# First mixture: three nested further tiles of an expert instead of six, and the branch hints given to all five engines

## The chip, the cores and the metric

One core of one Trainium2 chip. The metric is the device time of one execution in microseconds (us). Three runs of the kernel before took 1198.63, 1197.80 and 1197.21 us; their median is 1197.8 us. One more execution was taken with the hardware profiler; it is the one whose rows are shown.

## The reference, cut to what matters

```
x   = attention(q, k, v)                 # 4 batches x 576 rows = 2304 tokens of 512 numbers
# first mixture: 8 experts, F = 1024, not every token takes part
on  = x @ w_skip > 0
e   = argmax(x[on] @ w_gate)             # one expert a token
x[on] += gate * relu(x[on] @ w1[e]) @ w2[e]
# second mixture: 4 experts, F = 1024, every token through every expert
p   = domain_probs / sum(domain_probs)
out = sum over e of p[e] * (relu(x @ v1[e]) @ v2[e])
```

With these inputs 807 tokens take part in the first mixture; the eight experts get 7, 9, 127, 179, 459, 16, 2 and 8 of them. In tiles of 128 rows that is one tile for each expert, one further tile for expert 3 and three further tiles for expert 4: twelve tiles in all. The kernel can't know these counts ahead.

## The kernel before, in words

The kernel has three stages: attention and routing, to about 230 us of the profiled execution; the first mixture (`m1`), to about 410 us; and the second mixture, to the end. Every product in fp32 is made of three matmuls of a high and a low part, so ScalarE and VectorE split each operand (`parts`, `w_split`) before TensorE can use it.

**Routing.** Each token that takes part is written to a place in a region `XS` in DRAM, which holds the rows of each expert one behind the other. `counts` (line 489) counts the tokens of each expert on TensorE and works out on VectorE, in `row` (line 154, `[128, CM, 8]` int32), the first row of each further tile c, for c from 1 to CM - 1.

**A tile of the first mixture** (`m1_tile`): the rows of a tile are loaded, turned by four transposes on TensorE (`turned`, line 692), split, multiplied by w1 (line 710) and w2 (line 729), and the result is added to the row by VectorE into `ys` (line 737). GpSimd then writes `ys` to the tokens' places in `XN` by an indirect DMA, the put (line 738). There are two `ys` buffers (`YB = 2`). While a tile runs, `mid` turns and splits the rows of the tile that comes after it.

**The loop over experts** is unrolled. For each expert the first tile always runs. Then `more(1, x1)` opens a nested `tc.If` (line 803): the further tile c runs where the count is above 128 * c, and inside it stands the If of tile c + 1. For c below CM = 6 the further tile first loads the rows of tile c + 1, gives a hint on the next branch and turns those rows in `mid`, whether or not tile c + 1 will run. The tile at c = CM has none of that. Behind it stands a loop, without a hint, for the tiles that are left; with 459 rows it never runs. An expert's way out is thus a taken branch past the code of all further tiles that it doesn't need. Only behind the If comes `out()`, which adds and puts the expert's first tile. So the engines go past each branch in their own time, and meet again where data, or a buffer, is needed.

They tell the engine's sequencer early which way a branch with that label will go. There is one ahead of each first tile and one in each further tile with c below CM.

**Weights.** Weights come by SP's queue through a ring of raw tiles; as soon as a split frees one, the next load starts (`fetch`, `sp`). ScalarE and VectorE split them between the tiles' own work (lines 661 and 662).

## Time and profile before

| | us |
|---|---|
| median of three runs | 1197.8 |
| profiled execution, its own time | 1193.83 |
| its span (first to last instruction) | 1192.2 |
| VectorE's addition into `ys`, first and last start | 254.0 and 409.7 |
| TensorE busy from 443 to 1192 us | 743.43 of 749 |
| TensorE busy over the span | 1108.0 |

The span is from the first to the last instruction of the profiled execution; 1.6 us lie around it. Times in rows are in us from the span's start. PE is TensorE (PEld its weight loads, PEq or PEldq its sequencer, which runs branches and waits), DVE is VectorE, ACT ScalarE, POOL GpSimd, SP SyncE. In a row in order of time the bracket tells how long the engine had been idle and what ended the wait.

### The profile page before, as it was taken

The numbers are of one execution on the slowest core, as the hardware profiler recorded it, in microseconds if no ns is written. First come the engines' busy times: TensorE is split into PE (matmuls) and PEld (weight loads), VectorE is DVE, ScalarE is ACT, GpSimd is POOL, SyncE is SP. The second block draws the span as 40 slices with busy tenths as digits, with TensorE's granted clock in tenths as the row PEclk, the third lists the DMA queues.
The fourth block names the chain that finished last, engine by engine and source line by source line (L and its number), as shares of the span: only waits on it lengthen the run. The fifth ranks groups of instructions, "written<-read, shape, count | busy, mean of one in ns | idle before, by whom it ended". The sixth has DMA issues, their size and how long they took to land.

```text
span 1192.2 us, 19617 instructions
## 1 busy us (share of the span) xinstructions
PE 1108.0 (93%) x7485; PEld 973.3 (82%) x7485; DVE 767.6 (64%) x1227; ACT 505.9 (42%) x827; POOL 577.6 (48%) x579
## 2 busy tenths in 40 slices
PE   5889888699898779999999999999999999999998
PEld 4778887588797668988898998889888888888887
DVE  6767676578525676666666666666866667666665
ACT  5887785376425553332323233322533333333331
POOL 5968775101111065445454444545666555555551
PEclk8998899599999989999999999999999999999999
DMA  5998849499824331111111111111322111111101
GB/s 188 206 204 194 184 111 227 152 316 368 266 91 155 102 133 54 36 36 36 54 36 44 45 37 36 36 54 36 124 72 70 53 54 48 59 36 57 50 1 70
DMA packets 127248, 123.07 MB, mean 103 GB/s; under 512 B 63341, under 2 KB 96109, under 8 KB 127120
## 3 DMA queue, kind: packets, MB, share of 16 engines
q1 hardware_dynamic: 124400, 116.82, 33.8%
q0 software_dynamic: 2720, 4.64, 1.1%
q8 instruction: 69, 1.13, 0.4%
q14 instruction: 59, 0.48, 0.1%
HBM read 91.83 MB, written 19.43 MB: 93 GB/s over the span
## 4 chain that ended last, share of the span: by engine, by line
PE 62%; DVE 3%; POOL 1%; ACT 1%; DMA 0%; issue 0%; SPq 0%; POOLq 0%; ACTq 0%
PE yp L669 11%; PE yp L670 11%; PE yp L668 11%; PE hp L669 9%; PE hp L670 9%; PE hp L668 9%; DVE xsl L872 1%; PE hp L710 1%; PE yp L729 0%; DVE acc L1002 0%; DMA x<-XN 0%; PE tp L854 0%; DVE C L940 0%; POOL C L940 0%; POOL p L940 0%
## 5 line engine op out<-in xcount | busy, mean ns | idle before, releaser
L1002 DVE SCALAR_TENSOR_TENSOR acc<-yp,p,acc 128x512 f32<-128x512 f32 x270 | 199.1, 746 | 108.7 <-PE yp L670 108.6
L947 ACT ACTIVATE hh<-C 128x512 fp32r<-128x512 f32 (+2 forms) x98 | 81.7, 834 | 369.3 <-DVE C L940 328.8
L668 PE MATMUL yp<-vh,hh 128*128 128x512 f32 x576 | 226.6, 393 | 5.1 <-ACT hh L947 4.8
L669 PE MATMUL yp<-vl,hh 128*128 128x512 f32 x576 | 227.2, 394 | 1.0 <-POOL vl L917 1.0
L670 PE MATMUL yp<-vh,hl 128*128 128x512 f32 x576 | 226.4, 393 | 0.3 <-DVE hl L948 0.3
L948 DVE SCALAR_TENSOR_TENSOR hl<-C,hh 128x512 fp32r<-128x512 f32 (+2 forms) x98 | 93.2, 951 | 98.6 <-ACT hh L947 98.6
L940 POOL TENSOR_TENSOR p<-C,p 128x256 f32<-128x256 f32 (+2 forms) x49 | 50.4, 1029 | 199.4 <-ACT p L937 199.4
L670 PEld LDWEIGHTS yp<-vh,hl 128*128 128x128 f32 x576 | 108.7, 189 | 24.9 <-DVE hl L948 1.6
L668 PEld LDWEIGHTS yp<-vh,hh 128*128 128x128 f32 x576 | 109.0, 189 | 23.6 <-ACT hh L947 5.7
L669 PEld LDWEIGHTS yp<-vl,hh 128*128 128x128 f32 x576 | 109.0, 189 | 18.8 <-POOL vl L917 1.8
L917 POOL TENSOR_TENSOR vl<-r,vh 128x512 fp32r<-128x512 f32 x64 | 83.1, 1310 | 79.3 <-ACT vh L914 79.3
L940 DVE TENSOR_TENSOR C<-hp,p 128x256 f32<-128x256 f32 (+2 forms) x147 | 80.0, 544 | 35.6 <-PE hp L670 13.9
L669 PE MATMUL hp<-xsl,th 128*128 128x256 f32 (+2 forms) x294 | 97.9, 333 | 1.5 <-DVE xsl L872 1.5
L668 PE MATMUL hp<-xsh,th 128*128 128x256 f32 (+2 forms) x294 | 97.8, 333 | 0.0
L670 PE MATMUL hp<-xsh,tl 128*128 128x256 f32 (+2 forms) x294 | 97.8, 332 | 0.0
L738 POOL DMA_INDIRECT XN<-ys,xg x10 | 14.7, 1469 | 139.5 <-DVE ys L737 91.2
L302 ACT ACTIVATE E<-s,m 128x320 f32<-128x320 f32 (+4 forms) x160 | 75.9, 532 | 10.6 <-DVE m L295 9.2
L335 POOL TENSOR_TENSOR HL<-E,HL 128x1152 bf16<-128x1152 f32 (+2 forms) x37 | 63.7, 1737 | 21.9 <-ACT HL L334 14.6
L295 DVE TENSOR_REDUCE m<-s 128x1 f32<-128x576 f32 (+3 forms) x80 | 64.9, 819 | 14.1 <-PE s L286 12.6
L940 POOL TENSOR_TENSOR C<-C 128x256 f32<-128x256 f32 (+2 forms) x49 | 52.5, 1070 | 36.1 <-ACT C L937 34.8
L668 PE MATMUL hp<-xdh,dh 128*128 128x256 f32 (+2 forms) x196 | 65.1, 332 | 1.2 <-ACT xdh L861 1.2
L669 PE MATMUL hp<-xdl,dh 128*128 128x256 f32 (+2 forms) x196 | 65.2, 333 | 0.3 <-DVE xdl L862 0.3
(215 smaller groups left out, 2866.6 us busy)
## 6 DMA issues: line engine op xcount, KB each, us to landing
r<-in_w_dram SPq DMA_DIRECT2D x128, 512.0 KB, 5.8
XN<-x SPq DMA_DIRECT2D x18, 256.0 KB, 3.8
vr<-in_v_dram SPq DMA_DIRECT2D x7, 640.0 KB
xg<-XS SPq DMA_DIRECT2D x16, 257.0 KB, 5.7
out_dram<-acc SPq DMA_DIRECT2D x16, 256.0 KB, 2.0
qr<-in_q_dram SPq DMA_DIRECT2D x7, 576.0 KB, 7.4
kr<-in_k_dram SPq DMA_DIRECT2D x7, 576.0 KB, 6.4
x<-XN SPq DMA_DIRECT2D x12, 256.0 KB, 4.0
```

What stands on the lines that cost most here:

```text
L295: nc.vector.tensor_reduce(mo, mi, axis=ax, op=ALU.max, negate=True)
L302: nc.scalar.activation(e, views[j], AF.Exp, bias=m[:R, c:c + 1])
L335: (nc.vector if item[:2] in self.HV else nc.gpsimd).tensor_tensor(HL[:R, w:2 * w].bitcast(BF16), Et[:R, 0:w], HL[:R, 0:w], ALU.subtract)
L668: nc.tensor.matmul(out, lhsT=ah, rhs=bh, start=start, stop=False)
L669: nc.tensor.matmul(out, lhsT=ah, rhs=bl, start=False, stop=False)
L670: nc.tensor.matmul(out, lhsT=al, rhs=bh, start=False, stop=stop)
L738: nc.gpsimd.indirect_dma_start(out=self.XN, out_offset=bass.IndirectOffsetOnAxis(ap=xg[:, DM:DM + 1].bitcast(I32), axis=0), in_=ys, in_off ...
L917: nc.gpsimd.tensor_tensor(vl[:, f], r2[:, f], vh[:, f].bitcast(F32), ALU.subtract)
L940: add = lambda e, o, x, y: e.tensor_tensor(o, x, y, ALU.add)
L947: nc.scalar.activation(hh, C[:, i:i + 2], AF.Relu)
L948: V.scalar_tensor_tensor(hl, C[:, i:i + 2], 0.0, hh.bitcast(F32), ALU.max, ALU.subtract)
L1002: nc.vector.scalar_tensor_tensor(a, yp, self.p[:, n, e:e + 1], a, ALU.mult, ALU.add)
```

## The change

`CM` goes from 6 to 3, and the list of engines that get the hints goes to `None`, which stands for all five engines.

```
-    CM = 6
+    CM = 3
...
-        en = [mybir.EngineType.PE, mybir.EngineType.Activation, mybir.EngineType.DVE]
+        en = None
```

So the program holds, for each expert, the code of a first tile, three nested further tiles and the loop, instead of a first tile, six and the loop. The row tile is `[128, 3, 8]` instead of `[128, 6, 8]`, and `counts` fills two row numbers instead of five. The third further tile is now the one at c = CM: it loads and turns no rows of a fourth, and gives no hint; the test for a fourth tile is now that of the loop, without a hint. GpSimd and SyncE get the instructions of the hints too.

## Rows read from the trace of the kernel before

**Rows 1.** The page, part 1: busy time, share of the span, instructions.

```profile
PE 1108.0 (93%) x7485; PEld 973.3 (82%) x7485; DVE 767.6 (64%) x1227; ACT 505.9 (42%) x827; POOL 577.6 (48%) x579
```

**Rows 2.** Busy time by stretch: PE, PEld, DVE, ACT, POOL; clock, DMA share, GB/s.

```profile
365.10:383.30 18.20, 14.57 (x84) 12.55 (x85) 11.81 (x12) 10.17 (x14) 2.72 (x2) 0.91 0.56 184
443.00:1192.00 749.00, 743.43 (x3764) 645.01 (x3763) 487.25 (x691) 237.41 (x381) 382.12 (x374) 1.00 0.15 49
```

**Rows 3.** Instructions of line 737: count, ns min/median/max, first and last start.

```profile
L737 DVE SCALAR_TENSOR_TENSOR ys<-yp,xg x10: 750/751/752, 254.0 to 409.7; 128x512 f32<-128x512 f32 x10
L737 DVE SCALAR_TENSOR_TENSOR ys<-yp,xi x2: 751/752/752, 351.6 to 364.3; 128x512 f32<-128x512 f32 x2
```

**Rows 4.** TensorE and ScalarE in order: start, us busy, engine, work [idle us before <-releaser].

```profile
252.50 0.35 PE L710 MATMUL hp<-w1h,hi 128*128 128x256 f32 x1 [0.64 <-PEq L803]
280.51 0.38 PE L710 MATMUL hp<-w1h,hi 128*128 128x256 f32 x1 [1.10 <-ACTq L803]
280.80 2.00 ACT L661 CAST w2h<-r 128x1024 fp32r<-128x1024 f32 x2 [1.51 <-ACTq L803]
309.80 0.36 PE L710 MATMUL hp<-w1h,hi 128*128 128x256 f32 x1 [1.85 <-PEq L803]
319.32 0.63 PE L692 MATMUL tp<-ident,h 128*128 128x128 f32 x4 [1.72 <-DVE lo L685]
365.12 0.36 PE L710 MATMUL hp<-w1h,hi 128*128 128x256 f32 x1 [0.89 <-PEq L803]
375.89 0.63 PE L692 MATMUL tp<-ident,h 128*128 128x128 f32 x4 [2.98 <-DVE lo L685]
```

**Rows 5.** Instructions of line 803, the branches, whole run, ns min/median/max.

```profile
L803 PEldq COMPARE_BRANCH  x14: 68/350/4494, 248.6 to 406.4; - x14
L803 SPq COMPARE_BRANCH  x14: 34/45/53, 258.3 to 403.6; - x14
L803 POOLq INC_SWDGE_SEM  x8: 537/697/813, 234.7 to 404.5; - x8
```

**Rows 6.** The same line from 299 to 309.2 us: expert 3's way out.

```profile
L803 PEldq COMPARE_BRANCH  x1: 4494/4494/4494, 304.3 to 304.3; - x1
```

**Rows 7.** TensorE in the last further tile of expert 4.

```profile
357.58 0.60 PE L692 MATMUL tp<-ident,xi 128*128 128x128 f32 x4
357.94 0.48 PE L729 MATMUL yp<-w2h,hi 128*128 128x512 f32 x1
```

**Rows 8.** Line 737 from 305 to 314 us: VectorE's wait on semaphores.

```profile
L737 DVEq EVENT_SEMAPHORE  x3: 50/50/3809, 309.2 to 313.2; - x3
```

**Rows 9.** VectorE in order of time, behind the further tiles.

```profile
307.99 0.75 DVE L737 SCALAR_TENSOR_TENSOR ys<-yp,xg 128x512 f32<-128x512 f32 x1 [3.07 <-PE yp L729]
313.29 0.75 DVE L737 SCALAR_TENSOR_TENSOR ys<-yp,xg 128x512 f32<-128x512 f32 x1 [4.55 <-DMA XS<-x,sl]
369.85 0.75 DVE L737 SCALAR_TENSOR_TENSOR ys<-yp,xg 128x512 f32<-128x512 f32 x1 [4.83 <-DMA XN<-ys,xi]
370.52 4.62 DVE L662 TENSOR_TENSOR w2l<-r,w2h 128x1024 fp32r<-128x1024 f32 x4
```

**Rows 10.** GpSimd in order of time, the same two places.

```profile
309.02 1.02 POOL L738 DMA_INDIRECT XN<-ys,xg  x1 [23.98 <-DVEq L803]
365.30 1.00 POOL L738 DMA_INDIRECT XN<-ys,xi  x1 [11.01 <-DVEq L803]
```

**Rows 11.** Line 788, the hints: TensorE's row of three alike.

```profile
L788 PEldq ALU_OP  x12: 37/37/48, 235.6 to 396.8; - x12
```

**Rows 12.** VectorE's row numbers, and what TensorE waits for at the stage's start.

```profile
230.15 0.50 DVE L499 SCALAR_TENSOR_TENSOR row<-t,base 128x8 int32<-128x8 f32 x5
235.54 1.08 PE L692 MATMUL tp<-ident,xg 128*128 128x128 f32 x4 [5.70 <-DMA xg<-XS]
```

**Rows 13.** TensorE behind the wait at 375.89, and the granted clock there.

```profile
377.59 1.91 PE L729 MATMUL yp<-w2h,lo 128*128 128x512 f32 x4
381.61 1.07 PE L729 MATMUL yp<-w2h,lo 128*128 128x512 f32 x4
378.00:380.00 2.00, 2.00 (x6) 1.61 (x5) 1.84 (x2) 2.00 (x4) 0.00 (x0) 0.50 1.01 364
```

## The prediction

> **What bounds the kernel now.** I read the page's busy shares first: TensorE is busy for 1108.0 us, 93% of the span, and no other engine comes near [rows 1]. Then the stretches: from 443 us to the end TensorE is busy for 743.43 of 749.00 us at full clock [rows 2]. The change touches nothing that runs there; the second mixture only starts earlier or later. The additions of line 737 show where the first mixture lies and what it does: twelve tiles between 254.0 and 409.7 us; the two that take their rows from `xi` are the second and third further tile of expert 4 [rows 3]. TensorE is the engine that ends this stage too, so only its waits there count. Last I read TensorE in order of time around each branch [rows 4]. An ordinary way past a first tile's branch costs it 0.64 us (252.50). Four places cost more:
> - 280.51: 1.10 us, where ScalarE was late (it too had waited for its branch, 1.51 us).
> - 309.80: 1.85 us, expert 3's way out.
> - 319.32: 1.72 us, for a `lo` of VectorE.
> - 365.12 and 375.89: 0.89 us on expert 4's way out, and 2.98 us for another `lo`.

> These five idle times are 1.10 + 1.85 + 1.72 + 0.89 + 2.98 = 8.5 us; the change can't win more than a part of these, and the weight splits between keep their length.

> **Part 1, the third further tile loses its look-ahead.** It no longer turns rows of a fourth tile. TensorE's four transposes stand from 357.58, and the next matmul starts at 357.94 [rows 7]: 0.36 us on TensorE's path, in a stretch where it has no wait. Bounds: nothing if the next tile's split is then what TensorE waits for, 0.60 us if the transposes' whole busy time goes. I take -0.36. The load of those rows, one of GpSimd's, and its split on ScalarE and VectorE go as well; TensorE doesn't wait for them, so I take nothing.

> **Part 2, shorter code to jump over.** TensorE's branch on expert 3's way out took 4494 ns [rows 6], while the median of the fourteen is 350 ns [rows 5]. TensorE itself lost only 1.85 us [rows 4], because its queue still held matmuls: about 4.49 - 1.85 = 2.64 us of it were hidden. With three bodies fewer behind it, the target lies nearer, and the long branch should become an ordinary one; expert 4's, also on the way past skipped bodies, cost 0.89. So 1.85 becomes about 0.9: -0.95. But this doesn't reach the end. What comes next, at 319.32, waits for VectorE [rows 4], and VectorE didn't wait for TensorE: `out()` of expert 3 stands behind a semaphore wait of 3809 ns [rows 8] that ended just before 313.29 [rows 9]. The two `ys` buffers explain it: the further tile's `ys` (307.99, 0.75 us) is read by the put that GpSimd issues at 309.02 for 1.02 us [rows 10], and `out()` comes to the same buffer. Expert 4 repeats it: `ys` at 364.3 [rows 3], put at 365.30 [rows 10], `out()` at 369.85, then four weight splits of 4.62 us from 370.52 [rows 9], then the `lo` TensorE waited 2.98 us for [rows 4]. The number of skipped bodies doesn't alter which buffer `out()` gets, as I read the nesting: the allocation inside the If is undone behind it. So the put's landing stays on the path, and 0.95 us saved at 309.80 are waited again at 319.32. I take 0; bounds 0 and -0.95.

> **Part 3, GpSimd's catching-up.** On a way out an engine has to make up for the signals of the DMAs it skipped. GpSimd's do it with instructions of 537 to 813 ns, median 697 [rows 5]. Behind expert 3's put there are fewer skipped DMAs with three bodies less, and I expect VectorE to wait for the landing alone, about one such instruction earlier: -0.7 (bounds 0 and -0.81). At expert 4 fewer bodies are skipped already, and I take its wait as unchanged.

> [...]

> **Part 4, ScalarE's late branch.** At 280.51 TensorE waited 1.10 us for ScalarE, which had waited 1.51 us for its own branch [rows 4]. With shorter code to jump over, this should become the ordinary 0.64: -0.46. It could as well appear at another expert, since the bodies shift: bounds -0.46 and +0.46. I take -0.46.

> **Part 5, edits at nothing.** `counts` loses three of five operations of together 0.50 us, 0.3 us of VectorE [rows 12]. TensorE's next work, at 235.54, waited 5.70 us for a load of rows, which comes after the puts of the rows and not after these numbers [rows 12]: hidden; without that cover it would win 0.3 us. The hints: TensorE's row shows twelve instructions of 37 to 48 ns [rows 11], three alike. GpSimd and SyncE get eleven of them each; TensorE, ScalarE and VectorE lose one, since the third tile gives no hint. GpSimd's only work in this stage is loads and puts, and it had been idle for 23.98 us before the put of 309.02 [rows 10]; SyncE's branches took 34 to 53 ns without hints [rows 5], so there is nothing for a hint to win on that engine. I take 0. No row shows a hint on these two engines; from TensorE's row it is 11 x 2 x 48 ns = 1.1 us if all of it fell on the path, and 0 otherwise. The smaller row tile moves what is laid out behind it by 96 bytes; no row tells what that does, and I take 0.

> **Sum.** -0.36 + 0 - 0.7 - 0.46 = -1.5 us. The profiled execution, 1193.83 us (a span of 1192.2 and 1.6 around it), becomes 1192.3. It was 4.0 us shorter than the median of the runs; the same difference carried over, 1197.8 becomes **1196.3**. The bounds together give -0.60 - 0.95 - 0.81 - 0.46 - 0.3 = -3.1 and +0.46 + 1.1 = +1.6: 1194.7 to 1199.4.

> **Rival A: the wait for the put goes (faster).** If `out()` gets the other `ys` buffer when three bodies are gone, VectorE stops waiting at both ways out, and TensorE loses the 1.72 and 2.98 us [rows 4], as well as a slow clock: behind the wait of 2.98, four matmuls took 1.91 us that later take 1.07, at a granted clock of 0.50 [rows 13], and the stretch has a mean of 0.91 [rows 2], that is 18.20 x 0.09 = 1.6 us. With 0.95 no longer swallowed, and 0.36 and 0.46: -8.1 us, 1189.7. For it: the wait is the largest one. Against it: the first further tile and `out()` meet in one buffer today at expert 3 (one body ran) and at expert 4 (three), both odd numbers, and the code ran past is no body. Chance 0.10.

> **Rival B: the saved stall lowers the clock.** If expert 3's way out gets shorter but VectorE is not earlier, the 1.72 us at 319.32 become 2.67, nearly the 2.98 behind which the clock fell to 0.50 [rows 13]. Then 1.6 us are lost there and part 3 gives nothing: -0.36 - 0.46 + 1.6 = +0.8, 1198.6. For it: the waits' sizes. Against it: GpSimd's shorter catching-up takes the wait back to 1.97. Chance 0.12. [...]

> **Rival C: the hints and the new layout make more branches late (slower).** [...] Today one of TensorE's fourteen branches is late, for 4494 ns, at a price of 1.85 - 0.64 = 1.2 us [rows 4, 6]. A branch costs extra once it outlasts the queued matmuls, some 2.64 + 0.64 = 3.3 us. With one late branch the gain holds no more; with three of the first tiles' branches late it is 3 x 1.2 = +3.6 on the sum, 1199.9, and with six 1203.5. For it: one branch of fourteen is late today with everything else alike, so the place of the code does decide. Against it: shorter jumps. Chance 0.10.

> **Rival D: it does nothing that counts.** The 4494 ns branch stays because its cause is not the length of the code, ScalarE's stays, and the 0.36 us are eaten by the put of expert 4: 1197.8 - 0.4 = 1197.4 to 1197.8. Chance 0.13.

> **How the numbers follow.** The forecast has 0.55, with its own range 1194.0 to 1199.4; A 0.10, B 0.12, C 0.10, D 0.13. For the range I leave out A's full size and C's with more than three late branches, and keep the case in which only expert 4's wait goes (-2.98 - 1.6 - 0.8 = -5.4, 1192.4): 1192.4 to 1199.9. A difference of 0.2%, 2.4 us, is about the least that a measurement of this kernel can tell from none. Faster by more: 0.10 from A and four tenths of 0.55, 0.32. Slower by more: 0.10 from C and 0.03 from the upper bounds, 0.13. Within: 0.55.

> **What would show it.** Right: expert 3's branch on TensorE under 1000 ns and the idle time at its way out about 0.9; the `lo` wait behind it about 2.0; VectorE's wait of 3809 ns shorter by some 0.7; expert 4's wait still near 3 us with the clock at 0.50 behind it; no transposes between lines 710 and 729 in its last tile. Wrong: both waits for `lo` gone (A), a clock of 0.50 behind expert 3's way out (B), more than one TensorE branch over 3.3 us (C), or a difference in attention or the second mixture, which the sum holds unchanged.

## The result, and the profile after

The changed kernel takes 1206.23 us (median of 11 runs) against 1196.6 us for the kernel before, beside it on one chip: a ratio of 1.0069, 95% interval 1.0044 to 1.0095. Measured a second time beside the kernel before it was 1.0105 (1.0071 to 1.0138). The forecast was 1196.3 us, the range 1192.4 to 1199.9. The change makes the kernel slower by 0.4 to 1.4%, and its time lies outside the range.

The page of the changed kernel's profiled execution. In the queues' lines: packets, MB, share of the 16 engines.

```profile
span 1205.1 us, 19506 instructions
...
PE 1116.2 (93%) x7481; PEld 980.4 (81%) x7481; DVE 767.0 (64%) x1223; ACT 505.4 (42%) x826; POOL 575.5 (48%) x578
...
q8 instruction: 76, 1.25, 0.5%
q14 instruction: 50, 0.40, 0.1%
```

The span grew by 12.9 us. Line 737 tells where: its first addition starts 0.9 us later than in [rows 3], its last 12.5 us later, and from that one to the end of the span it is 782.9 us against 782.5. The loss, 11.6 us, lies between the first and the last addition of the first mixture.

```profile
L737 DVE SCALAR_TENSOR_TENSOR ys<-yp,xg x10: 750/751/751, 254.9 to 422.2; 128x512 f32<-128x512 f32 x10
L737 DVE SCALAR_TENSOR_TENSOR ys<-yp,xi x2: 750/751/752, 361.7 to 374.0; 128x512 f32<-128x512 f32 x2
```

The first thing to look for is the row of [rows 11]. The trace after has no row on line 788, and none of the hint instructions themselves: with `None` for the list **no engine gets a hint**, where the words of the change (and my prediction) have all five get them. What that does is in TensorE's branches of line 803, which answer to [rows 5]:

```profile
L803 PEldq COMPARE_BRANCH  x12: 65/3433/6452, 249.6 to 419.0; - x12
```

The median went from 350 to 3433 ns. Now TensorE in order of time, at the ways out of experts 0 to 6, behind which the next expert's first matmul waits as in [rows 4] (the first, at 253.65, costs 0.76 us):

```profile
270.52 0.55 PE L710 MATMUL hp<-w1h,hi 128*128 128x256 f32 x1 [3.70 <-PEq L803]
275.20 0.58 PE L710 MATMUL hp<-w1h,hi 128*128 128x256 f32 x1 [3.48 <-issue]
290.92 0.36 PE L710 MATMUL hp<-w1h,hi 128*128 128x256 f32 x1 [1.13 <-PEq L803]
318.74 0.35 PE L710 MATMUL hp<-w1h,hi 128*128 128x256 f32 x1 [0.70 <-PEq L803]
320.94 0.58 PE L710 MATMUL hp<-w1l,hi 128*128 128x256 f32 x1 [1.13 <-issue]
374.65 0.36 PE L710 MATMUL hp<-w1h,hi 128*128 128x256 f32 x1 [0.69 <-PEq L816]
390.78 0.36 PE L710 MATMUL hp<-w1h,hi 128*128 128x256 f32 x1 [3.13 <-PEq L803]
395.48 0.79 PE L710 MATMUL hp<-w1h,lo 128*128 128x256 f32 x2 [3.28 <-issue]
409.67 0.36 PE L710 MATMUL hp<-w1h,hi 128*128 128x256 f32 x1 [0.78 <-PEq L803]
```

Read the rows in pairs. "PEq L803" is the wait at the branch: 3.70 us behind expert 1, 3.13 behind expert 5, and about 0.7 to 1.1 elsewhere; all seven come to 10.9 us. "issue" is a second wait, soon behind three of the branches, with nothing in the trace that TensorE waits for: 3.48 + 1.13 + 3.28 = 7.9 us. Behind the long waits the clock is down, as the granted clock (first number behind POOL; the traces of both kernels hold 1.00 and 0.50 and no other value) of the windows there shows:

```profile
270.50:271.70 1.20, 1.18 (x4) 0.92 (x4) 0.42 (x1) 1.20 (x2) 0.43 (x1) 0.50 1.09 349
275.20:279.85 4.65, 4.65 (x22) 4.65 (x22) 0.00 (x0) 0.00 (x0) 0.00 (x0) 0.50 1.06 381
320.94:324.30 3.36, 3.36 (x16) 3.36 (x16) 2.41 (x3) 0.00 (x0) 1.48 (x2) 0.50 0.48 133
395.48:399.30 3.82, 3.82 (x18) 3.82 (x19) 0.00 (x0) 0.37 (x1) 0.00 (x0) 0.50 0.02 4
```

By the clock alone these 13.0 us at 0.50 hold 6.5 us of work, so some 6.5 us are lost, an estimate; by the starts of the 128x256 matmuls, 0.213 us apart there and 0.119 behind 280.0, where the clock is 1.00, it is 5.7. But something was also won, and it is not small. VectorE at the places of [rows 9]:

```profile
318.08 0.75 DVE L737 SCALAR_TENSOR_TENSOR ys<-yp,xg 128x512 f32<-128x512 f32 x1 [3.06 <-PE yp L729]
320.33 0.75 DVE L737 SCALAR_TENSOR_TENSOR ys<-yp,xg 128x512 f32<-128x512 f32 x1 [1.50 <-DMA XS<-x,sl]
373.99 0.75 DVE L737 SCALAR_TENSOR_TENSOR ys<-yp,xi 128x512 f32<-128x512 f32 x1 [3.34 <-PE yp L729]
376.39 0.75 DVE L737 SCALAR_TENSOR_TENSOR ys<-yp,xg 128x512 f32<-128x512 f32 x1 [1.65 <-DMA XN<-ys,xg]
```

Expert 3's further tile and `out()` start 2.25 us apart, not 5.30; expert 4's 2.40, not 5.6. Both waits for `lo`, 1.72 and 2.98 us in [rows 4], are gone. What is left of VectorE's wait at expert 3 is 891 ns, in place of the 3809 of [rows 8], and it ends as GpSimd's catching-up ends (319.6 + 0.63):

```profile
L737 DVEq EVENT_SEMAPHORE  x2: 50/470/891, 319.3 to 320.2; - x2
L803 POOLq INC_SWDGE_SEM  x1: 634/634/634, 319.6 to 319.6; - x1
```

The sum for this execution, against 6.4 us for the same seven branches before (0.64, 0.63 and 0.69 at the three whose rows aren't shown): first waits +4.5, second waits +7.9, clock +6.5 - 1.6 = +4.9, `lo` -4.7, look-ahead -0.4: +12.2, where 11.6 were measured.

### The profile page after: what moved, and what is told of

Its sections match the earlier page's. It is cut to its first block, busy times and chain, and to the rows that moved or that the text cites. A ratio compares the mean times of both kernels' runs of the same rounds, so it can differ in the third digit from the quotient of the medians.

```text
span 1205.1 us, 19506 instructions
## 1 busy us (share of the span) xinstructions
PE 1116.2 (93%) x7481; PEld 980.4 (81%) x7481; DVE 767.0 (64%) x1223; ACT 505.4 (42%) x826; POOL 575.5 (48%) x578
## 4 chain that ended last, share of the span: by engine, by line
PE 60%; issue 3%; DVE 2%; DMA 2%; POOL 1%; ACT 1%; SPq 0%; POOLq 0%; ACTq 0%
PE yp L669 11%; PE yp L670 11%; PE yp L668 11%; PE hp L669 9%; PE hp L670 9%; PE hp L668 9%; DMA XN<-ys,xg 2%; DVE xsl L872 1%; PE tp L854 1%; DVE acc L1002 0%; DVE xdl L862 0%; POOL p L940 0%; ACT hh L947 0%; DVE C L940 0%; POOL vl L917 0%
## 5 line engine op out<-in xcount | busy, mean ns | idle before, releaser
L738 POOL DMA_INDIRECT XN<-ys,xg x10 | 12.6, 1262 | 154.2 <-DVE ys L737 87.7
```

What stands on the lines that cost most here:

```text
L738: nc.gpsimd.indirect_dma_start(out=self.XN, out_offset=bass.IndirectOffsetOnAxis(ap=xg[:, DM:DM + 1].bitcast(I32), axis=0), in_=ys, in_off ...
```

## The experiments

The experiments were measured in three groups, each on one chip and with runs of the kernel before in it. Only ratios are compared across groups, since the kernel before takes 1189 to 1190 us in these and 1196.6 us beside the first measurement of the changed kernel.

| kernel | tiles nested | hints on | ratio to before, 95% |
|---|---|---|---|
| the change, first measurement | 3 | none | 1.0069 (1.0044 to 1.0095) |
| the change, again | 3 | none | 1.0105 (1.0071 to 1.0138) |
| old hints | 3 | PE, ACT, DVE | 0.9957 (0.9933 to 0.9980) |
| no hints | 6 | none | 1.0065 (1.0039 to 1.0090) |
| five named | 3 | all five | 0.9940 (0.9916 to 0.9964) |
| own `ys` buffers | 6 | PE, ACT, DVE | 0.9941 (0.9916 to 0.9965) |
| code moved | 3 | none | 1.0041 (1.0019 to 1.0062) |
| five tiles | 5 | PE, ACT, DVE | 0.9957 (0.9937 to 0.9976) |
| four tiles | 4 | PE, ACT, DVE | 1.0004 (0.9979 to 1.0030) |
| TensorE's hints alone | 3 | PE | 0.9944 (0.9927 to 0.9961) |
| the other two's alone | 3 | ACT, DVE | 1.0031 (1.0010 to 1.0052) |

**Only the first half: three tiles, the old hints.**

```
-    CM = 6
+    CM = 3
```

> Only the first half of the change: three nested further tiles, the hints still on TensorE, ScalarE and VectorE. Theory H (with the list None no engine gets a hint at all, and every way past a body makes TensorE wait 3.4 to 6.5 us for code): TensorE's long branches are gone here, median near 350 ns as before. Theory B (with an odd number of bodies out() gets the other ys buffer, so VectorE no longer waits for the put): the 1.72 and 2.98 us for lo stay away, and so does the low clock behind the second. H and B together: about 8 us faster than before, 1187 to 1191. Rival S (the shorter code, or where it comes to lie, makes the branches late): slow as the changed kernel, 1203 to 1208. My recorded sum (no buffer gained): 1195.

1182.65 us against 1189.17, by the ratio of 0.9957 some 5.1 us faster; H and B hold (the largest wait for `lo` left is 0.19 us), S falls. The gain is smaller than the 8 us expected; one branch of TensorE is late here in spite of its hint (TensorE's wait is 1.83 us, behind expert 1), and the next one shows the ordinary 0.64 where [rows 4] had 1.10 with ScalarE late:

```profile
L803 PEldq COMPARE_BRANCH  x12: 68/347/4343, 239.3 to 391.4; - x12
```

```profile
258.10 0.36 PE L710 MATMUL hp<-w1h,hi 128*128 128x256 f32 x1 [1.83 <-PEq L803]
273.33 0.36 PE L710 MATMUL hp<-w1h,hi 128*128 128x256 f32 x1 [0.64 <-PEq L803]
```

**Only the second half: six tiles, no hints.**

```
-        en = [mybir.EngineType.PE, mybir.EngineType.Activation, mybir.EngineType.DVE]
+        en = None
```

> Only the second half of the change: six nested further tiles, the list of engines None. H: no hint row in the trace, TensorE's ways past bodies take 3.4 to 6.5 us, of which some 3.3 are hidden; the low clock behind the longest adds to it. With B, the changed kernel is 9.6 us slower in spite of 8 us won, so the hints' loss is near 17 us: 1209 to 1216, the waits for lo still there. Rival S: about as before, 1195 to 1199.

1196.3 us, 1.0065, so 7.7 us slower: the direction is H's, the size is not, 12 us or more had been expected. TensorE's branches are as late as in the changed kernel:

```profile
L803 PEldq COMPARE_BRANCH  x14: 65/3550/6194, 241.3 to 406.4; - x14
```

The first waits come to 12.3 us, 5.9 more than before; the clock stands at 0.50 for 9.1 us of work behind the two longest and, by the clock alone as above, loses some 2.9 us more than before, and the waits for `lo` are 1.0 us shorter: 7.8 us, in line with the 7.7. What is missing is the second kind of wait: no "issue" stands behind a way out here. The kernel with its code moved, below, asks why.

**All five engines, named.**

```
-        en = None
+        en = [mybir.EngineType.PE, mybir.EngineType.Activation, mybir.EngineType.DVE, mybir.EngineType.Pool, mybir.EngineType.SP]
```

> What the change says in words: three nested tiles, and the hints on all five engines, each named in the list. H and B: hint rows on all five engines; GpSimd and SyncE aren't waited for at these places, so as the kernel with three tiles and the old hints, within 1.5 us: 1187 to 1191. [...]

1183.0 us, 0.9940, the same as with three engines within the intervals; GpSimd and SyncE get their hints here (rows of the hint instructions, ns min/median/max). What the change says in words is a gain of 0.4 to 0.8%; what it does is the opposite. Two branches of TensorE were late (4.1 and 4.4 us) in this execution, one with three engines, so rival C may happen in small, and it doesn't decide.

```profile
L1215 POOLq BRANCH_PREFETCH_HINT  x11: 28/35/63, 229.6 to 390.6; - x11
L1215 PEldq BRANCH_PREFETCH_HINT  x11: 27/40/40, 231.4 to 387.0; - x11
L1215 SPq BRANCH_PREFETCH_HINT  x11: 28/31/56, 248.3 to 375.7; - x11
```

**Six tiles, the two buffers given out otherwise.**

```
-        ys = self.wk.tile([128, 512], F32, tag="y", bufs=self.YB, name="ys")
+        ys = self.wk.tile([128, 512], F32, tag="s" + y, bufs=1, name="ys")
```

(`y` is handed through from `m1_tile`: "y" for an expert's first tile, "yi" for the further ones.)

> The kernel before, six nested tiles and the old hints, but the two ys buffers are given out otherwise: one for the first tiles' out(), one for all further tiles. The code's length and the hints stay. B: VectorE's wait of 3809 ns and the one behind expert 4 go; TensorE wins 1.72 + 2.98 us and the 1.6 us of the low clock, and may keep expert 3's late branch: about 6 us faster than before, 1189 to 1192. Rival P (the wait is for the put's semaphore, used again by the DMAs of the bodies skipped, whatever the buffer): no change, 1195 to 1199.

1181.97 us, 0.9941: 7.0 us faster than the kernel before, with the same code length, the same hints and the same space. VectorE goes from a further tile to `out()` in 1.35 and 1.33 us, sooner than the 2.25 and 2.40 us of the changed kernel. P falls: the wait is tied to the buffer that `out()` gets.

```profile
305.42 0.75 DVE L737 SCALAR_TENSOR_TENSOR ys<-yp,xg 128x512 f32<-128x512 f32 x1 [3.09 <-PE yp L729]
306.77 0.75 DVE L737 SCALAR_TENSOR_TENSOR ys<-yp,xg 128x512 f32<-128x512 f32 x1 [0.59 <-DVEq L803]
359.11 0.75 DVE L737 SCALAR_TENSOR_TENSOR ys<-yp,xi 128x512 f32<-128x512 f32 x1 [3.32 <-PE yp L729]
360.44 0.75 DVE L737 SCALAR_TENSOR_TENSOR ys<-yp,xg 128x512 f32<-128x512 f32 x1 [0.57 <-DVEq L803]
```

**Five and four tiles, the old hints** (`CM = 5`, `CM = 4`).

> Five nested further tiles and the old hints. Theory B: with an odd number of bodies out() gets the other ys buffer; the waits for lo behind experts 3 and 4 go, 5 to 8 us faster than before, as with three bodies (0.994 to 0.996). Rival N (it is the number of bodies or skipped DMAs that counts, not odd or even): between six and three, 0 to 2 us faster.

> Four nested further tiles and the old hints. Theory B: an even number, out() shares the buffer with the tile whose put has just gone out; VectorE's waits of some 3.8 us stay, and the time is that of the kernel before within 2 us. Rival N: nearer to three bodies, 3 to 6 us faster than before.

Five: 1182.43 us, 0.9957. Four: 1189.82 us, 1.0004. In the times odd is fast and even is not, as B has it; N would have four between. (With five, two branches are late in spite of their hints, 4.6 us ahead of 301.06 and 3.8 us behind expert 5, and take a part back.) With five tiles no wait for `lo` is left behind expert 4, and expert 3's is 0.29 us:

```profile
301.06 0.36 PE L710 MATMUL hp<-w1h,hi 128*128 128x256 f32 x1 [1.95 <-PEq L803]
310.60 0.63 PE L692 MATMUL tp<-ident,h 128*128 128x128 f32 x4 [0.29 <-DVE lo L685]
```

But at expert 3 that isn't because `out()` came sooner. VectorE's wait is still there: 5.42 us from the further tile to `out()`, where the kernel before had 5.30. TensorE only reached the place later, with its clock at 0.50 from 302.22 to 305.63; the transposes that wait for `lo` start 9.5 us behind the first matmul in both kernels. Expert 3 with five tiles, with GpSimd's put and its catching-up:

```profile
299.14 0.75 DVE L737 SCALAR_TENSOR_TENSOR ys<-yp,xg 128x512 f32<-128x512 f32 x1 [3.07 <-PE yp L729]
300.17 1.02 POOL L738 DMA_INDIRECT XN<-ys,xg  x1 [23.49 <-DVEq L803]
L803 POOLq INC_SWDGE_SEM  x1: 617/617/617, 303.8 to 303.8; - x1
304.56 0.75 DVE L737 SCALAR_TENSOR_TENSOR ys<-yp,xg 128x512 f32<-128x512 f32 x1 [4.67 <-DMA XS<-x,sl]
```

The catching-up starts 3.6 us behind the put's issue (before: 3.5, with four tiles 0.6, with three 0.5); the wait that GpSimd ends ahead of it with five names the semaphore of that put. With three, five and six tiles VectorE goes on when the catching-up ends (320.2 and 320.33 us with three, 304.4 and 304.56 with five, 313.1 and 313.29 with six). In the changed kernel it stands once at each of the eight ways out: seven times on line 803, and on line 816 for expert 4, which skips the loop's tile alone. So there are two ways by which `out()` stands behind the put: the buffer, and GpSimd's catching-up for the bodies skipped. At expert 3 the catching-up is clear of the put with four tiles or fewer, odd or even, as N would have it; at expert 4 the catching-up of the kernel before ends at 366.7 us, and `out()` comes at 369.85 all the same, so there the buffer decides.

With four tiles both waits for `lo` are there:

```profile
313.77 0.63 PE L692 MATMUL tp<-ident,h 128*128 128x128 f32 x4 [2.92 <-DVE lo L685]
371.17 0.63 PE L692 MATMUL tp<-ident,h 128*128 128x128 f32 x4 [2.45 <-DVE lo L685]
```

No trace names the buffers. The waits fit this order: the further tiles take the buffers in turn, the loop's tile takes the next, and `out()` gets **the loop's tile's** buffer. With six the order is 0, 1, 0, 1, 0, 1, loop 0, `out()` 0, so `out()` stands on the buffer of tiles 1 and 3; with three it is 0, 1, 0, loop 1, `out()` 1.

**The changed kernel again, and with its code moved.** Sixteen matmuls of 8 columns were put ahead of the stage, where TensorE waits for a load (5.70 us in [rows 12]):

```
+        pad = self.ps_t.tile([128, 4, 128], F32, tag="t", name="pad")
+        for _ in range(16):
+            nc.tensor.matmul(pad[0:8, 0, 0:8], lhsT=self.ident[:, 0:8], rhs=self.ident[:, 0:8], start=True, stop=True)
```

> The changed kernel itself, so that the kernels of this call are compared with it on one chip. As before: 0.5 to 0.9% slower than the kernel before, TensorE's waits of 3 to 4 us at the same three experts (1, 3 and 5), 4, 7 and 10 matmuls behind the branch.

> The changed kernel with 16 tiny matmuls more on TensorE ahead of the first mixture, where it waits for a load anyway: their results are used by nothing, they move all later code on by 64 instructions. Theory L: without hints, the code behind a branch comes in pieces; in the changed kernel the ways out of experts 1, 3 and 5 land 10, 16 and 22 instructions ahead of the next piece (4, 7 and 10 matmuls), so TensorE waits again (3.48, 1.13 and 3.28 us), and twice the low clock follows. Moved by 64, no expert lands within 70 instructions ahead of a piece: the second waits go, the first ones of 0.8 to 3.7 us stay: 7 to 11 us faster than the changed kernel, about as the kernel before (-2 to +3 us). Rival M (the second wait comes from the saturated DMA queues or the wait itself, wherever the code lies): second waits stay, as the changed kernel within 2 us.

The changed kernel: 1202.35 us, 1.0105, a little more than the 0.5 to 0.9% expected. Its seven first waits are 12.6 us, its second waits 4.35 + 1.40 + 2.26 = 8.0 us, behind the same three experts, 4, 7 and 10 matmuls behind the branch. Moved: 1193.53 us, by the ratios 7.6 us less (0.0064 of 1189), or 3.3 us less by the first measurement of the changed kernel; 4.9 us slower than the kernel before, where 3 at most had been expected. Its first waits are 12.5 us, no less than before; its second waits are 0.92 and 0.71 us (at 253.60 and 290.97), now behind experts 0 and 2 and each 26 matmuls behind the branch:

```profile
253.60 0.28 PE L710 MATMUL hp<-w1h,hi 128*128 128x256 f32 x1 [0.92 <-issue]
267.11 0.55 PE L710 MATMUL hp<-w1h,hi 128*128 128x256 f32 x1 [3.81 <-PEq L806]
285.43 0.35 PE L710 MATMUL hp<-w1h,hi 128*128 128x256 f32 x1 [2.97 <-PEq L806]
290.97 0.28 PE L710 MATMUL hp<-w1h,hi 128*128 128x256 f32 x1 [0.71 <-issue]
383.71 0.36 PE L710 MATMUL hp<-w1h,hi 128*128 128x256 f32 x1 [2.38 <-PEq L806]
```

**Which engine's hints** (the list `[PE]`, and the list `[Activation, DVE]`).

> The changed kernel with the hints given to TensorE alone. Theory H1 (only TensorE's late code costs time, since its branch comes last): as three tiles with the three old engines, 0.993 to 0.998 of the kernel before, TensorE's branches mostly under 1 us. Rival H3 (ScalarE's and VectorE's branches are late without hints as well, and TensorE waits for them): between that and the changed kernel, 1.000 to 1.006.

> The changed kernel with the hints given to ScalarE and VectorE, not to TensorE. H1: as the changed kernel, 1.006 to 1.012, TensorE's branches 3.4 to 6.5 us and its waits 4, 7 and 10 matmuls behind the ways out of experts 1, 3 and 5. H3: 2 us or more faster than the changed kernel, below 1.006.

TensorE alone: 1182.68 us, 0.9944, the whole gain, although three of its branches were late (4.2, 4.2 and 4.9 us). H1 holds and H3 has nothing left to explain:

```profile
L803 PEldq COMPARE_BRANCH  x12: 68/354/4904, 240.7 to 394.0; - x12
```

The trace of the changed kernel shows why the other two engines don't matter. Without hints too, no branch of ScalarE takes over 50 ns, and none of VectorE over 72:

```profile
L803 ACTq COMPARE_BRANCH  x12: 34/45/50, 248.3 to 417.6; - x12
L803 DVEq COMPARE_BRANCH  x12: 43/56/72, 252.7 to 418.2; - x12
```

ScalarE and VectorE alone: 1193.85 us, 1.0031. This missed both of H1's numbers: the ratio lies below 1.006, which was H3's sign, and no second wait stands behind experts 1, 3 or 5. The first waits are as long as ever (14.4 us in all, not less than the 12.6 without hints), so the two engines' hints took nothing off TensorE's branches:

```profile
L803 PEldq COMPARE_BRANCH  x12: 65/3544/6500, 240.0 to 403.8; - x12
```

```profile
261.00 0.41 PE L710 MATMUL hp<-w1h,hi 128*128 128x256 f32 x1 [3.60 <-PEq L803]
279.40 0.55 PE L710 MATMUL hp<-w1h,hi 128*128 128x256 f32 x1 [3.87 <-PEq L803]
379.27 0.36 PE L710 MATMUL hp<-w1h,hi 128*128 128x256 f32 x1 [3.67 <-PEq L803]
```

TensorE runs as many instructions as in the changed kernel, but its pieces begin elsewhere. Counted back from the end in TensorE's weight loads, two of the last pieces are fetched with 292 and about 165 to go in the changed kernel (both its traces), and with 315 and 187 here; over all pieces of the second mixture their edges lie some 21 weight loads, or 42 instructions, earlier. So the missing second waits fit L. Why the edges moved stays open. That ScalarE and VectorE have more code here is not enough: with three tiles the edges lie at the same places whether TensorE alone has hints (317 and 193 to go) or ScalarE and VectorE as well (316 and 193). And sixteen matmuls, 32 weight loads in the trace, moved them by 49.

## Why the prediction was wrong

**The step that failed, and that made it slower: part 5, "GpSimd and SyncE get eleven of them each".** I took the list `None` for five engines, looked only for what two more could cost, and put the hints at 0, at most +1.1 us. The trace of before shows hints on three engines [rows 11], and no row can tell what `None` does; that the change might *take* the hints was no rival of mine, though "doesn't do what it says" was the question to ask. With three tiles the loss by it is from 0.9957 to 1.0069 or 1.0105, that is 13 to 18 us.

**Part 2, the late branch.** A part of its mechanism was right: a late branch of TensorE, where a packet of q8 starts only behind it, takes 3.4 to 6.6 us, and what outlasts the queued matmuls is lost; they hide 2.5 to 2.9 us in the traces without hints, 2.64 in my working. I tied it to the length of the code. The runs tie it to the hint: six tiles with hints, median 350 ns; three without, 3433. The sign that I had named for rival C came, more than one branch over 3.3 us, though not by its cause: no engine had a hint. Its price was 1.2 us for each; here two cost 2.5 to 3.1 us more, and a second wait and the lowered clock, which that price did not hold, come to more than that.

**Part 2's other step, "the allocation inside the If is undone behind it".** By the waits it is not: expert 4's goes with three and with five tiles and stays with four and six, as if `out()` took the buffer of the loop's tile. Rival A, at 0.10, was what three tiles do: -8.1 us in my working, 5 to 7 us by the kernels with hints, where a late branch or more take a part back. My argument against it, that one body and three are both odd, counted the bodies that run, where those that are built decide.

**Part 3** had the right engine and kept the wrong half. With fewer bodies skipped, GpSimd's catching-up no longer stands behind the put, so at expert 3 the landing left VectorE's path and the catching-up stayed on it: 3809 ns became 891, some 2.9 us less, not 0.7. At expert 4, where I had no change, VectorE's idle time went from 4.83 to 1.65 us. **Part 1**: the four transposes are gone from the last further tile, and 0.4 us are too small to be measured by themselves. **Part 4** came in the kernel with three tiles and the old hints, 0.64 us at 273.33, but that way out takes 1.97 us with five engines' hints and 1.76 with TensorE's alone, where TensorE's own branch was late, and 1.13 without hints. **Rival B** did not come by its own cause: the clock fell behind expert 3's way out (320.94), yet behind a second wait for code. The forecast's own range stands once as 1194.7 and once as 1194.0 us at its lower end; its bounds add up to 1194.7, and nothing hangs on it.

## What to carry to other kernels

Where a change names an option, count in the trace what the option emits; a default may mean "none", as here. Give an If its hint on the engine whose branches turn out long without it, here TensorE (median 3433 ns without, 354 with its own hints alone): this one gave the whole gain (0.9944). Behind a nested If, look at which rotating buffer the code after it gets, and at what it waits for, expert by expert: a shorter wait further on may have another cause. Two tags of one buffer each gave as much (0.9941) as the shorter code with hints, and beat both kernels.

## What the runs showed of the hardware that was not expected

A branch without a hint could cost twice here: once for the piece of code it lands in (first waits of 0.7 to 3.9 us), and once more where TensorE came to the next piece soon, 4 to 10 matmuls behind (1.1 to 4.4 us; 0.7 and 0.9 us at 26). Two kernels in which the pieces' edges lay otherwise (sixteen tiny matmuls ahead, or hints on ScalarE and VectorE alone) were 0.3 to 0.7% faster than the changed one, by which of its two measurements is taken. And a hint did not always help: in the kernels with hints on TensorE none to three of its branches still took 3.5 to 4.9 us, and in each of these the packet of code started only behind the branch (before: hint at 290.9, branch at 304.3, packet at 306.2 us). All branches of TensorE over 2.9 us, in all traces, end 2.3 to 3.7 us after such a packet starts; for those of 3.3 to 4.0 us it starts 0.9 to 1.6 us behind the branch, for those over 6 us 2.8 to 4.0. What holds the packet up there, and at which hints, the runs leave open.
